# Fewer unread products in the opening, an earlier exp table, and batch 2 loaded through the software queue

## The chip, the cores and the metric

The kernel runs on one core of one Trainium2 chip. The metric is the time of one execution on the device in microseconds (us); before the change it was 310.43 us, the median of 8 runs (309.83 to 311.7).

The core has a matrix engine (TensorE, PE in the profile), VectorE (DVE), ScalarE (ACT), GpSimd (POOL) and SyncE (SP). Each works through its own list of instructions in order and waits for the others by semaphores. Sixteen DMA engines move data; GpSimd issues transfers into a software queue, which can also change float32 to bfloat16 on the way, and SyncE into a hardware queue, which can also transpose.

## The reference

Two stages follow each other. The first is attention over q, k and v of shape 8 x 8 x 576 x 64 (batches, heads, tokens, head size), in float32. For heads 0 to 3 a token sees itself and the 31 before it; for heads 4 to 7 it sees itself and every earlier token at a distance that 32 divides:

```python
mask_local = (rel >= 0) & (rel < stride)
mask_strided = (rel >= 0) & (pos[None, :] % stride == pos[:, None] % stride)
scores = np.where(masks[None, :, :, :], scale * q @ k^T, -1e9)
attn = softmax(scores);  x = (attn @ v) as 4608 tokens x 512
```

The second is a two-layer network over the 4608 tokens: `h = x @ w_in` (512 to 2048), Mish (`h * tanh(log1p(exp(h)))`), and `g @ w_out` (2048 to 512).

## The kernel before

**Blocks.** The tokens pass through the network in nine blocks of 512, t = 0 to 8. For each block `mlp1` makes the hidden layer in 8 groups of two 128-wide columns, 8 matmuls each (L557), and ScalarE applies Mish to each group (L563). `mlp2` makes the output (L580) in 16 pieces of 4 matmuls. Between the pieces of `mlp2` of block t stand the steps of the attention of batch t+1, written out by hand in `attn_steps` as a list `at`: the steps of `at[i]` follow piece i. So the order on TensorE is the order of the calls; there is no scheduler.

**Attention of a batch.** The strided heads ("s") are cut into 8 groups of 72 tokens, the local heads ("l") into 6 windows of 96 tokens. `qk` makes scores in a pair of PSUM banks (`acc`, three pairs in all) and ScalarE takes their exp (L339), which needs the exp table: ScalarE holds one table at a time, and Exp and Mish lie in different ones. `mask` multiplies by the mask on VectorE (L347). `pv` and `pv2` multiply by v, whose 65th column is ones, so that the sum of the weights comes along; VectorE divides by it (L374, L375; in `pv2` L388, L389). `xt` transposes the result on TensorE and copies it into `xT`, the input of `mlp1`. Batches 0 and 1 also have their q and k transposed on TensorE (`t_step`, `t_step_loc0`), with a copy out of PSUM behind each; the transposes share two small PSUM buffers (`tile_t`) with `pv`. From batch 2 on, q and k are transposed by DMAs of SyncE (`str_by_dma`, `loc_by_dma`).

**The opening.** Batch 0's attention runs before any block. TensorE has little to do there, and between its steps stand calls of `fill` (L526): products of a zeroed tile `kTs[1]` that nobody reads, 512 columns each. There are seven calls with 9, 4, 2, 2, 4, 2 and 2 products. The first waits for the memset of `kTs[1]` (L629).

**Loads.** GpSimd issues the loads of batches 0 and 1, of all weights, and of the strided q and k of every batch, in the order of the calls. A transfer that it issues waits for the eighth transfer before it. In the program of before, batch 2's local q and k and its v come by SyncE in float32 (`load_qk_loc`, `load_v`), and GpSimd casts them (`cast_qk_loc`, `cast_v`). A small transfer `gate` (L718), which reads a piece of `w_out`, stands ahead of them in SyncE's queue and so holds them back until that piece of `w_out` has landed. Behind them in the same queue stand the six transposing transfers of batch 2 (called in `at[9]` of block 0), and behind these the output of block 0 and the loads of batch 3. The function `next_loads`, called in `at[2]` of block 0, holds GpSimd's part: a copy of rows of v of batch 1 (windows overlap by 32 rows), the casts of batch 2 and the loads of batch 3's strided q and k.

**Block 0.** Its pieces run with `fc_major`, so that the four 128-token tiles of the output are all open at once and hold two PSUM pairs. The scores of batch 1 have only the third pair: the next part of the scores can start when exp has read the last.

Of the kernel before, what the change touches and what calls it, by code (L numbers as in the profile page):

```python
# [11 lines left out]
BF16 = mybir.dt.bfloat16  # L12
AF = mybir.ActivationFunctionType
# [4 lines left out]
WQ = 96  # L18
CL, PL = 6, 96
SU = 80  # L20
CS, PN = 8, 72
# [19 lines left out]
def kernel(ctx, tc, q, k, v, moe_w_in, moe_w_out, out):  # L41
    nc = tc.nc
    B, H, S, D = q.shape
# [9 lines left out]
    const = ctx.enter_context(tc.tile_pool(name="const", bufs=1))  # L53
    w_in = const.tile([128, 4, DF], BF16, name="w_in")
    w_out = const.tile([128, 16, DM], BF16, name="w_out")
# [11 lines left out]
    ql = [const.tile([128, CL, 4, D], BF16, name=f"ql{i}") for i in range(2)]  # L67
    kl = [const.tile([128, CL, 4, D], BF16, name=f"kl{i}") for i in range(2)]
    qs = [const.tile([128, 4, CS * D], BF16, name=f"qs{i}") for i in range(2)]
    ks = [const.tile([128, 4, CS * D], BF16, name=f"ks{i}") for i in range(2)]  # L70
    vl = [const.tile([128, NW, 4, D + 1], BF16, name=f"vl{i}") for i in range(2)]
# [4 lines left out]
    kTs = [const.tile([128, 16 * SU + 48], BF16, name=f"kTs{i}") for i in range(2)]  # L76
    P_s = [const.tile([PN, 2, n * PN + 56], BF16, name=f"Ps{i}") for i, n in enumerate((7, 7, 4))]
    P_l = [const.tile([128, 2, n * WQ + 32], BF16, name=f"Pl{i}") for i, n in enumerate((5, 5, 2))]
    gate = const.tile([1, 256], BF16, name="gate")
    x_l = const.tile([128, NW, 256], BF16, name="x_l")  # L80
    x_s = const.tile([128, CS, 256], BF16, name="x_s")
    xs_t = const.tile([128, CS, 2, 96], BF16, name="xs_t")
# [12 lines left out]
    def tile_t(name):  # L95
        return ps_t.tile([128, 512], F32, tag="pt", name=name)
# [18 lines left out]
    def load_qk_loc(b):  # L115
        for dst, src in ((kl32, k), (ql32, q)):
            nc.sync.dma_start(
                dst[0:PL].rearrange("p h i d -> p (h i) d"),
                src[b, 0:4].rearrange("h (i p) d -> p (h i) d", p=PL),
            )  # L120
# [6 lines left out]
    vsd = [vsd[:, 2048 * i:2048 * i + 2048] for i in range(2)]  # L127

    def load_v_str01(b):
        dst = vsd[b].rearrange("p (h x) -> p h x", h=4)  # L130
        if b == 0:
            load_str01(dst, v, b)
        else:
            nc.gpsimd.dma_start(dst, v[b, 4:8].rearrange("h (p j) d -> p h (j d)", j=CS))

    def load_v_loc01(b, w0, w1):
        for w in range(w0, w1):
            nc.gpsimd.dma_start(
                vl[b][32:128, w, :, 0:D], v[b, 0:4, WQ * w:WQ * w + WQ].rearrange("h p d -> p h d")
            )  # L140

    def rows_v_loc01(b, w0, w1, eng):
        w0 = max(w0, 1)
        cast(eng, vl[b][0:32, w0:w1, :, 0:D], vl[b][96:128, w0 - 1:w1 - 1, :, 0:D])

    def copy_v_str01(b, eng, j0, j1):
        cast(
            eng, vs[b][0:PN, :, j0:j1, 0:D],
            vsd[b].rearrange("p (h j d) -> p h j d", h=4, j=CS)[:, :, j0:j1, :],
        )  # L150

    def load_v_str(b):
# [9 lines left out]
    def load_v(b):  # L162
        load_v_str(b)
        load_v_loc(b)
# [13 lines left out]
    def cast(eng, out_, in_):  # L178
        if eng is nc.scalar:
            nc.scalar.copy(out_, in_)  # L180
        else:
            eng.tensor_copy(out_, in_)  # L182

    def cast_qk_loc(b, e_k, e_q):
        for e, dst, src in ((e_k, kl, kl32), (e_q, ql, ql32)):
            to = by_tile(dst[b % 2])
            for hp in range(2):
                cast(
                    e, to[:, hp].rearrange("p i e d -> p e i d"), src[0:PL, 2 * hp:2 * hp + 2]
                )  # L190

    def by_tile(x):

        return x[0:PL].rearrange("p j h d -> p (j h d)").rearrange(
            "p (t i e d) -> p t i e d", t=2, i=NW, e=2
        )
# [16 lines left out]
    def cast_v(b, e_s, e_l):  # L213
        cast(e_s, vs[b % 2][0:PN, :, :, 0:D], vs32[0:PN])
        cast_v_loc(b, e_l)
# [33 lines left out]
    def t_step_loc0(src, dst, hp, eng):  # L249

        tr = tile_t("tr")[:].bitcast(BF16)
        for j in range(CL):
            for e in range(2):
                nc.tensor.transpose(  # L254
                    tr[64 * e:64 * e + 64, PL * j:PL * j + PL], src[0:PL, 2 * hp + e, j, :],
                    ident[0:PL, 0:PL],
                )
        cast(
            eng, dst.rearrange("c (p j) -> c p j", j=CL),
            tr[:, 0:S].rearrange("c (j p) -> c p j", j=CL),  # L260
        )
# [5 lines left out]
    def t_steps1():  # L267
        r = [lambda w=w, hp=hp: t_step(1, w, hp) for hp in range(2) for w in ("k", "q")]
        kq = [
            (x[:].rearrange("p h (j d) -> p h j d", d=D), d)  # L270
            for x, d in ((rows(kl[1]), kTl[:, :, 32:32 + S]), (rows(ql[1]), qTl[:]))
        ]
        return r + [
            lambda x=x, d=d, hp=hp: t_step_loc0(x, d[:, hp, :], hp, nc.vector)
            for hp in range(2) for x, d in kq
        ]


# [247 lines left out]
    def fill(t, n):  # L526

        for _ in range(n):
            nc.tensor.matmul(  # L529
                t[:, 0:512], lhsT=kTs[1][:, 512:640], rhs=kTs[1][:, 0:512], start=True, stop=True  # L530
            )

    def fill_acc(i, n):
        fill(acc(i, "fill")[:, 0, :], n)
# [82 lines left out]
    with tc.manual_schedule():  # L617
# [8 lines left out]
        load_v_str01(0)  # L626
        load_qk_loc01(0, kl0, ql0)
        kl0, ql0 = [x.rearrange("p h (j d) -> p h j d", d=D) for x in (kl0, ql0)]
        Dv.memset(kTs[1][:], 0.0)  # L629
        Dv.memset(vl[0][:, :, :, D:D + 1], 1.0)  # L630
        Dv.memset(vl[0][0:32, 0], 0.0)
        load_v_loc01(0, 0, 3)
# [20 lines left out]
                )  # L653

        a = Attn(0)
        fill_acc(2, 9)
        for hp in range(2):
            t_step(0, "k", hp, Sc if hp else Dv)
        a.bias("s", 0, 0)
# [1 line left out]
        for hp in range(2):  # L661
            t_step(0, "q", hp, Sc if hp else Dv)
        a.bias("s", 1, 1)
        fill_acc(2, 2)
        a.bias("s", 2, 2)
        for i in range(3):
            a.qk([("s", i)], i)
# [5 lines left out]
        t_step_loc0(kl0, kTl[:, 1, 32:32 + S], 1, Sc)  # L673
        a.pv2("s", 2, 1)
        a.pv2("s", 4, 2)
        fill_acc(0, 4)
        t_step_loc0(ql0, qTl[:, 0, :], 0, Sc)
        t_step_loc0(ql0, qTl[:, 1, :], 1, Sc)
        a.pv2("s", 6, 0)
        a.bias("l", 0, 1)  # L680
        fill(tile_t("fill"), 2)
        a.bias("l", 1, 2)
        a.qk([("l", 0)], 1)
        a.qk([("l", 1)], 2)
# [6 lines left out]
        load_v_str01(1)  # L691
        load_qk_loc01(1, rows(kl[1]), rows(ql[1]))
        load_w_out(1, 3)
        for h in range(4):
            nc.gpsimd.dma_start(
                vl[1][32:128, :, h, 0:D], v[1, h].rearrange("(w p) d -> p w d", p=WQ)
            )
        load_w_out(3, 4)
        a.bias("l", 2, 0)
        a.qk([("l", 2)], 0)  # L700
        a.xt("s", 0, Dv)
        a.xt("s", 1, Dv)
        Sc.preload_act_table(AF.Mish)
        fill(tile_t("fill"), 2)
        a.pv2("l", 0, 1)
        a.pv2("l", 2, 0)
        a.pv2("l", 4, 1)
# [5 lines left out]
        a.xt("l", 1)  # L713
        Dv.memset(vl32[0:32], 0.0)
        for x in (ks, qs):
            Po.memset(x[0][64:SU], 0.0)
        load_qk_str(2)
        nc.sync.dma_start(gate[:], w_out[0:1, 11, 0:256])  # L718
        load_qk_loc(2)

        def next_loads():
            rows_v_loc01(1, 0, 6, Po)
            load_v(2)
            cast_qk_loc(2, Po, Po)
            load_qk_str(3)
            cast_v(2, Po, Po)

        for t in range(NBLK):
            x, y, z = accs
            if t > 0:  # L730
                gT, g1 = mlp1(t, accs)
            ts, at, a1 = [], [], []
            if t == 0:
                ts, at = t_steps1(), attn_steps(1, y, y)
                at[2] += [lambda: copy_v_str01(1, nc.vector, 0, CS), next_loads] + ts[4:6]
                at[3] += ts[6:8]
                at[9] += [lambda: str_by_dma(2), lambda: loc_by_dma(2)]
                out_accs, accs = (z, x), (y, z, x)
            else:
                if t <= 2:  # L740
                    at = attn_steps(t + 1, x, y, z if t == 2 else None)
                elif t + 1 < B:
                    a1 = str_steps(t + 1)
                    at = loc_steps(t + 1, x, y)
                if t == 1:
                    at[9].append(lambda: str_by_dma(3))
                if t == 2:
                    Dv.memset(x_s[64:96], 0.0)
                if t + 2 < B:
                    at[9].append(lambda: loc_by_dma(t + 2))  # L750
                if 1 < t < B - 3:
                    at[9].append(lambda: str_by_dma(t + 3))
                out_accs, accs = (z, y), (z, x, y)
            for i, g in enumerate(g1):
                g()
                if i < len(a1):
                    for s in a1[i]:
                        s()
                if t == 0:
                    for n in {6: (0, 1), 7: (2, 3)}.get(i, ()):  # L760
                        ts[n]()
            if t > 0 and t + 2 < B:
                cast_qk_loc(t + 2, Po, Po)
                if 1 < t < B - 3:
                    load_qk_str(t + 3)
                if t < 3:
                    cast_v(t + 2, Po, Po)
                else:
                    at[5].append(lambda: cast_v(t + 2, Po, Po))
            if t == 1:  # L770
                load_qk_str(4)
            if t == NBLK - 1:
                mlp2_last(t, gT, (z, y, x))
                break
            for i, g in enumerate(mlp2(t, gT, out_accs, fc_major=(t == 0))):
                g()
                if i < len(at):
                    for s in at[i]:
                        s()
            if t + 3 < B:  # L780
                load_qk_loc(t + 3)
                if t == 1:
                    str_by_dma(4)
                load_v(t + 3)
# [30 lines left out]
```

## Time and profile before

| | |
|---|---|
| median of 8 runs | 310.43 us |
| the profiled execution | 309.83 us |
| its span, first to last instruction | 308.10 us |
| TensorE busy in the span | 297.2 us (96%) |
| ScalarE, VectorE, GpSimd busy | 181.0, 155.5, 101.8 us |
| first product of `mlp1` that runs on without a wait | 23.78 us |
| `mlp2` of block 0 with attention of batch 1 | 36.9 to 59.99 us |
| `mlp2` of block 1 with attention of batch 2 | 73.81 to 92.47 us |
| transposing transfers of batch 2, first to last issue | 55.33 to 72.17 us |

Times in the profile are microseconds from the first instruction, unless ns is written. A line of the timeline gives the start, the length, the engine, the line of the kernel, the operation, what it writes and reads, its shape and how often it follows itself; in brackets stands how long the engine had been idle before it, and what ended the idle time. PEld is TensorE's weight load. SPq and the DMA lines of POOL are issues of transfers, whose data lands later. Matmuls are pipelined and their ends are modelled, so a matmul's line looks longer than the time by which it moves the next.

### The profile page before, as it was taken

Reading aid. Unit: us, or ns where it says so; the run is one execution under the profiler, and the core shown is the slowest. Engines: PE = TensorE matmul, PEld = TensorE weight load, DVE = VectorE, ACT = ScalarE, POOL = GpSimd, SP = SyncE. Lnnn points to the kernel's source line nnn. Section 1 sums busy time; section 2 is a strip of 40 time slices with the busy share of each in tenths; the row PEclk is TensorE's granted clock in tenths of the full one; section 3 lists DMA queues with packets and bytes.
Section 4 is the critical chain, followed back from the end, with each engine's and each line's share of the span. In section 5 each row is a group of like instructions: output and inputs, shape, how many; then the busy total and the mean of one; then the engine's idle time right before and its main releaser. Section 6 shows DMA issues by size and latency. Waiting matters only on the chain.

```text
span 308.1 us, 5881 instructions
## 1 busy us (share of the span) xinstructions
PE 297.2 (96%) x2437; PEld 154.7 (50%) x2437; DVE 155.5 (50%) x375; ACT 181.0 (59%) x193; POOL 101.8 (33%) x116
## 2 busy tenths in 40 slices
PE   6989979999999999999999999999999999999995
PEld 2544545544554455444579654445444544444444
DVE  3670257400870066578787978797879850000000
ACT  5555533667537664768766876687668746216501
POOL 8782551660236024502790297028600000000000
PEclk9999999999999999999999999999999999999999
DMA  7999999998999999999979996898420120011011
GB/s 115 175 185 201 204 169 174 183 147 210 186 192 147 206 155 208 187 197 193 168 160 168 194 177 149 146 190 148 126 89 0 41 98 0 2 68 68 0 70 68
DMA packets 97346, 42.84 MB, mean 139 GB/s; under 512 B 79400, under 2 KB 91112, under 8 KB 97320
## 3 DMA queue, kind: packets, MB, share of 16 engines
q1 hardware_dynamic: 78856, 30.94, 55.8%
q0 software_dynamic: 18176, 11.28, 27.7%
q8 instruction: 19, 0.31, 0.5%
q10 hardware_dynamic: 288, 0.25, 0.3%
q14 instruction: 7, 0.06, 0.1%
HBM read 36.82 MB, written 9.44 MB: 150 GB/s over the span
## 4 chain that ended last, share of the span: by engine, by line
PE 90%; DVE 4%; DMA 2%; ACT 1%; issue 1%; POOL 1%; ACTq 0%; POOLq 0%
PE psh L557 40%; PE pso L580 34%; PE po L363 5%; PE pso L607 5%; PE ps L325 3%; DMA qs<-in_q_dram 2%; DVE x_l L375 1%; DVE x_s L375 1%; PE fill L529 1%; PE trx L402 1%; ACT Ps L339 1%; PE ps L298 1%; PE tr L238 1%; PE tr L254 1%; DVE rden L374 1%
## 5 line engine op out<-in xcount | busy, mean ns | idle before, releaser
L557 PE MATMUL psh<-xT,w_in 128*128 128x512 bf16 (+1 forms) x640 | 130.6, 358 | 1.0 <-ACT xT L180 0.7
L580 PE MATMUL pso<-w_out,gT 128*128 128x512 bf16 x512 | 121.7, 379 | 0.0
L563 ACT ACTIVATE gT<-psh 128x1024 bf16<-128x1024 f32 x72 | 72.4, 1023 | 47.3 <-PE psh L557 47.3
L557 PEld LDWEIGHTS <-w_in 128*128 128x128 bf16 x640 | 60.1, 98 | 56.5 <-issue 1.4
L580 PEld LDWEIGHTS <-gT 128*128 128x128 bf16 x512 | 45.4, 97 | 46.0
L182 POOL CAST kl<-kl 96x768 bf16<-96x768 f32 x12 | 9.9, 846 | 76.8 <-DMA kl<-in_k_dram 60.9
L437 DVE STREAM_TRANSPOSE xs_t<-x_s 32x512 bf16<-32x512 bf16 x48 | 33.7, 702 | 0.9
L587 ACT COPY osb<-pso 128x1024 f32<-128x1024 f32 x16 | 17.6, 1100 | 24.6 <-PE pso L580 14.0
L374 DVE RECIPROCAL rden<-po 72x4 f32<-72x4 f32 (+1 forms) x98 | 17.3, 176 | 26.2 <-PE po L363 26.0
L347 DVE TENSOR_TENSOR Ps<-Ps,consts_sb 72x864 bf16<-72x864 bf16 (+3 forms) x12 | 7.0, 583 | 41.7 <-ACT Ps L339 41.7
L428 DVE STREAM_TRANSPOSE xT<-x_l 32x384 bf16<-32x384 bf16 x48 | 27.3, 569 | 0.7
L182 DVE COPY osb<-pso 128x512 f32<-128x512 f32 (+1 forms) x2 | 1.1, 558 | 51.3 <-PE pso L607 51.3
L339 ACT ACTIVATE Ps<-ps 72x864 bf16<-72x864 f32 (+3 forms) x21 | 17.4, 860 | 13.3 <-PE ps L325 13.3
L375 DVE TENSOR_TENSOR x_s<-po,rden 72x256 bf16<-72x256 f32 x56 | 23.5, 420 | 1.9
L444 ACT COPY xT<-xs_t 128x576 bf16<-128x576 bf16 x8 | 21.4, 2941 | 0.0
L363 PEld LDWEIGHTS <-Ps 72*128 72x128 bf16 x256 | 14.9, 97 | 11.6 <-DVE Ps L347 0.8
L182 POOL CAST vl<-vl 128x768 bf16<-128x768 f32 (+2 forms) x24 | 18.5, 771 | 4.9 <-DMA vl<-in_v_dram 3.8
L339 ACT ACTIVATE Pl<-ps 128x960 bf16<-128x960 f32 (+1 forms) x20 | 17.1, 875 | 3.8 <-PE ps L325 3.8
L375 DVE TENSOR_TENSOR x_l<-po,rden 96x256 bf16<-96x256 f32 x42 | 17.6, 420 | 1.4
L180 ACT COPY xT<-trx 128x576 bf16<-128x576 bf16 x14 | 8.8, 639 | 15.4 <-PE trx L412 11.2
L363 PE MATMUL po<-vs,Ps 72*128 72x65 bf16 x256 | 17.4, 194 | 0.1
L182 POOL CAST ql<-ql 96x768 bf16<-96x768 f32 x12 | 10.3, 882 | 14.2 <-DMA ql<-in_q_dram 14.2
(86 smaller groups left out, 233.8 us busy)
## 6 DMA issues: line engine op xcount, KB each, us to landing
out_dram<-osb SPq DMA_DIRECT2D x16, 512.0 KB, 4.6
kl<-in_k_dram SPq DMA_DIRECT2D x6, 576.0 KB
ql<-in_q_dram SPq DMA_DIRECT2D x6, 576.0 KB, 11.6
vs<-in_v_dram SPq DMA_DIRECT2D x6, 576.0 KB
vl<-in_v_dram SPq DMA_DIRECT2D x6, 576.0 KB, 10.0
w_out<-in_moe_w_out_dram POOLq DMA_DIRECT2D x4, 512.0 KB, 15.2
ks<-in_k_dram POOLq DMA_DIRECT2D x7, 288.0 KB, 7.3
qs<-in_q_dram POOLq DMA_DIRECT2D x7, 288.0 KB, 8.4
```

Source lines behind the costliest of these rows:

```text
L182: eng.tensor_copy(out_, in_)
L339: nc.scalar.activation(pt[0:n, :, 0:nw], t[0:n, :, o0:o0 + nw], AF.Exp, scale=scale)
L363: nc.tensor.matmul(po[:, h, :], lhsT=pt[0:n, c0:c0 + 128], rhs=rhs, start=True, stop=True,)
L374: nc.vector.reciprocal(rden[0:m, :], po[0:m, :, D])
L375: nc.vector.tensor_tensor(out=dst.rearrange("p (h d) -> p h d", h=4), in0=po[0:m, :, 0:D], in1=rden[0:m, :].unsqueeze(2).to_broadcast([m, ...
L428: nc.vector.transpose(dst[32 * q:32 * q + 32, :, :, m:m + 32], src[m:m + 32, :, :, q, :])
L437: nc.vector.transpose(xs_t[32 * q:32 * q + 32, :, :, m:m + 32], src[m:m + 32, :, :, q, :])
L444: nc.scalar.copy(xT[:, 2 + c, t0:t0 + S].rearrange("p (n j) -> p j n", j=CS), xs_t[:, :, c, 0:PN])
L557: nc.tensor.matmul(ps[:, u, o:o + n], lhsT=w_in[:, cc, fc * 128:(fc + 1) * 128], rhs=xT[:, cc, a:a + n], start=(cc == 2 and o == 0), stop= ...
L563: nc.scalar.activation(gT[:, 2 * g:2 * g + 2, :], ps[:], AF.Mish)
L580: nc.tensor.matmul(p[:, ot % 2, :], lhsT=gT[:, fc, 128 * ot:128 * ot + 128], rhs=w_out[:, fc, :], start=(fc == 0), stop=(fc == 15),)
L587: nc.scalar.copy(osb[:], p[:])
```

## The change

It has three parts. In the opening, the memset of `kTs[1]` is cut in two, of which the first covers what `fill` reads; the numbers of unread products become 11, 4, 1, 2 and 1, and two calls go; the second copy of `xt("s", ...)` of batch 0 moves from VectorE to ScalarE. In block 0 the exp table is loaded behind piece 0 of `mlp2`, the copy of v and `next_loads` move from `at[2]` to `at[1]`, ahead of the mask, and the copies of the local q transposes of batch 1 move from VectorE to ScalarE. Batch 2's local q and k and its v are loaded by GpSimd's queue as bfloat16: the loads of q and k are one transfer for each head, and those of v are the functions of batch 1, which now take any batch. The gate, the float32 loads of batch 2 and its casts go; what stays on GpSimd is a copy of v's strided rows and the row copy. The memsets of the padding rows of `ks[0]` and `qs[0]` move from GpSimd to VectorE.

```diff
-    gate = const.tile([1, 256], BF16, name="gate")
...
+    def load_v_loc_h(b):
+        for h in range(4):
+            nc.gpsimd.dma_start(
+                vl[b % 2][32:128, :, h, 0:D], v[b, h].rearrange("(w p) d -> p w d", p=WQ)
+            )
...
-            lambda x=x, d=d, hp=hp: t_step_loc0(x, d[:, hp, :], hp, nc.vector)
-            for hp in range(2) for x, d in kq
+            lambda x=x, d=d, hp=hp, e=e: t_step_loc0(x, d[:, hp, :], hp, e)
+            for hp in range(2) for (x, d), e in zip(kq, (nc.vector, nc.scalar))
...
-        Dv.memset(kTs[1][:], 0.0)
+        Dv.memset(kTs[1][:, 0:640], 0.0)
+        Dv.memset(kTs[1][:, 640:], 0.0)
...
-        fill_acc(2, 9)
+        fill_acc(2, 11)
...
-        fill_acc(2, 2)
+        fill_acc(2, 1)
...
-        fill_acc(0, 4)
+        fill_acc(0, 1)
...
         a.bias("l", 0, 1)
-        fill(tile_t("fill"), 2)
         a.bias("l", 1, 2)
...
-        for h in range(4):
-            nc.gpsimd.dma_start(
-                vl[1][32:128, :, h, 0:D], v[1, h].rearrange("(w p) d -> p w d", p=WQ)
-            )
+        load_v_loc_h(1)
...
-        a.xt("s", 1, Dv)
+        a.xt("s", 1)
         Sc.preload_act_table(AF.Mish)
-        fill(tile_t("fill"), 2)
...
-            Po.memset(x[0][64:SU], 0.0)
+            Dv.memset(x[0][64:SU], 0.0)
         load_qk_str(2)
-        nc.sync.dma_start(gate[:], w_out[0:1, 11, 0:256])
-        load_qk_loc(2)
+        rows_v_loc01(1, 0, 6, Po)
+        for dst, src in ((kl, k), (ql, q)):
+            to = by_tile(dst[0])
+            for h in range(4):
+                nc.gpsimd.dma_start(
+                    to[:, h // 2, :, h % 2, :], src[2, h].rearrange("(i p) d -> p i d", p=PL)
+                )
+        load_v_str01(2)
+        load_v_loc_h(2)

         def next_loads():
-            rows_v_loc01(1, 0, 6, Po)
-            load_v(2)
-            cast_qk_loc(2, Po, Po)
             load_qk_str(3)
-            cast_v(2, Po, Po)
+            copy_v_str01(2, Po, 0, CS)
+            rows_v_loc01(2, 0, 6, Po)
...
-                at[2] += [lambda: copy_v_str01(1, nc.vector, 0, CS), next_loads] + ts[4:6]
+                at[0] += [lambda: Sc.preload_act_table(AF.Exp)]
+                at[1] += [lambda: copy_v_str01(1, nc.vector, 0, CS), next_loads]
+                at[2] += ts[4:6]
```

More of the change, by code (lines that the diff above doesn't have):

```diff
@@ L129, in load_v_str01 @@
     def load_v_str01(b):
-        dst = vsd[b].rearrange("p (h x) -> p h x", h=4)
+        dst = vsd[b % 2].rearrange("p (h x) -> p h x", h=4)
         if b == 0:
@@ L140, in load_v_loc01 @@
             )
+    def load_v_loc_h(b):
[3 more added lines that the diff above has]
+            )
     def rows_v_loc01(b, w0, w1, eng):
-        w0 = max(w0, 1)
-        cast(eng, vl[b][0:32, w0:w1, :, 0:D], vl[b][96:128, w0 - 1:w1 - 1, :, 0:D])
+        w0, x = max(w0, 1), vl[b % 2]
+        cast(eng, x[0:32, w0:w1, :, 0:D], x[96:128, w0 - 1:w1 - 1, :, 0:D])
     def copy_v_str01(b, eng, j0, j1):
         cast(
-            eng, vs[b][0:PN, :, j0:j1, 0:D],
-            vsd[b].rearrange("p (h j d) -> p h j d", h=4, j=CS)[:, :, j0:j1, :],
+            eng, vs[b % 2][0:PN, :, j0:j1, 0:D],
+            vsd[b % 2].rearrange("p (h j d) -> p h j d", h=4, j=CS)[:, :, j0:j1, :],
         )
```

## The prediction

> **What bounds the kernel now.** I read the page's busy shares first, then a table of busy time by stage, then the list of waits of TensorE alone, then the timeline where that table shows TensorE idle. The busy share names the engine:
>
> ```profile
> PE 297.2 (96%) x2437; PEld 154.7 (50%) x2437; DVE 155.5 (50%) x375; ACT 181.0 (59%) x193; POOL 101.8 (33%) x116
> ```
>
> TensorE fills 96% of the span, and all matmuls of the nine token blocks stay as they are. So a gain has to come from the 4% in which TensorE stands still, or from TensorE work without a reader. In the table of stages (columns: stretch; then busy of PE, PEld, DVE, ACT, POOL; granted clock; DMA) the stretches to look at are these:
>
> ```profile
> 10.00:20.00 10.00, 8.91 (x186) 5.74 (x184) 6.57 (x15) 7.22 (x10) 8.55 (x13) 1.00 1.48 172
> 20.00:23.80 3.80, 2.69 (x29) 1.64 (x30) 3.26 (x6) 1.46 (x3) 1.77 (x3) 1.00 1.24 207
> ...
> 37.00:60.00 23.00, 20.99 (x256) 11.81 (x253) 14.90 (x41) 10.10 (x13) 10.77 (x11) 1.00 1.42 179
> 60.00:73.80 13.80, 13.80 (x65) 6.27 (x64) 0.00 (x0) 9.24 (x9) 6.33 (x7) 1.00 1.03 151
> ```
>
> From 60 us on a stage is full (13.80 of 13.80). Before 24 us, and from 37 to 60 us, it is not; and part of what counts as busy before 24 us is the fill, which nobody reads. The timeline (start, length, engine, operation, idle before and its releaser) of the opening:
>
> ```profile
> 13.05 1.03 PE L529 MATMUL fill<-kTs 128*128 128x512 bf16 x4
> ...
> 15.31 0.59 PE L529 MATMUL fill<-kTs 128*128 128x512 bf16 x2
> ...
> 17.70 1.42 DVE L182 COPY xT<-trx 128x576 bf16<-128x576 bf16 x2 [1.65 <-PE trx L412]
> 18.51 0.59 PE L529 MATMUL fill<-kTs 128*128 128x512 bf16 x2 [0.59 <-DVE xT L182]
> ...
> 20.38 0.43 PE L363 MATMUL po<-vl,Pl 128*128 128x65 bf16 x8 [0.76 <-DVE x_l L389]
> ```
>
> Here a fill stands in TensorE's order ahead of work that could run: the last pair waits until VectorE has emptied a transpose buffer (18.44), and the local attention products behind it start only at 18.94. Then the first block's second projection:
>
> ```profile
> 36.59 1.02 ACT L563 ACTIVATE gT<-psh 128x1024 bf16<-128x1024 f32 x1 [1.23 <-PE psh L557]
> 39.19 1.28 ACT L339 ACT_TABLE_LOAD   x1 [1.58 <-PE ps L325]
> 40.49 0.89 ACT L339 ACTIVATE Ps<-ps 72x864 bf16<-72x864 f32 x1
> 41.42 0.37 PE L325 MATMUL ps<-qTs,kTs 64*128 64x72 bf16 x12 [1.35 <-ACT Ps L339]
> 42.53 0.75 DVE L182 COPY kTl<-tr 128x576 bf16<-128x576 bf16 x1
> 43.20 0.74 DVE L182 COPY qTl<-tr 128x576 bf16<-128x576 bf16 x1
> ```
>
> ScalarE is free from 37.61, but loads the exp table only when the scores are there (39.19). TensorE's next scores need the same PSUM pair, so TensorE stands 1.35 us.
>
> **The opening, part by part.** The first fill group grows from 9 to 11, and the memset it waits for is halved. Memsets of 664 and 64 words took 612 and 112 ns, 0.83 ns a word, so 320 words take about 325 ns: the fill starts at 0.95+0.33+0.06 = 1.34 instead of 1.62. Nine fills took 1.62 to 5.28, less the last's tail: loads 0.427 us apart. Eleven at that pace end at 1.34+11x0.427 = 6.03; the first keys release TensorE at 6.06. Cost 0.0, at most 0.1. The 4 and the 2 fills that stay are hidden by the query transfer and the first exp.
>
> Fill 2 to 1 before the third bias: the bias pair shares the fill's PSUM pair and started at 9.82, when the second fill had drained. One fill less is 0.22; the last query copy (to 9.64) does not bind. First exp: 10.56 to 10.34, and the chain behind moves 0.22.
>
> Fill 4 to 1 at 13.05: the local query transposes (14.01) then wait for their buffer, which VectorE's copy of the keys frees (12.81+0.74 = 13.55, less 0.22 = 13.33). They start near 13.38, 0.63 earlier. The fill pair at 15.31 goes: the bias behind it needs VectorE's read of a product (14.53+0.69 = 15.22, less 0.22 = 15.00), so it starts about 15.05 instead of 15.74, 0.69 earlier; the query copies, also 0.63 earlier, end at 15.05. The three local exps then run 15.98 to 18.19 (16.67 and 2.21 long before).
>
> The fill pair at 18.51 goes, and the second xT copy moves from VectorE to ScalarE. The first pair of products runs as soon as exp and transposes are done (17.1). VectorE has one copy (17.0 to 17.7) ahead of its division instead of two, and divides until 17.72+0.20+0.04+0.69 = 18.65. The second pair needs the third exp (18.19). The third pair needs the first division: 18.7 instead of 20.38. On ScalarE the moved copy runs 18.19 to 18.83 (0.64, its row elsewhere), then the Mish table to 20.11, before the next xT copy (about 20.5). From the third pair on the order of TensorE is the old one, with the same links (VectorE 0.88 per product, one transpose, one ScalarE copy): MLP1's free run starts at about 22.15 instead of 23.78. **Opening: -1.6.**
>
> Does the input keep up? Each transfer that GpSimd issues waits for the eighth before it, so its waits date the landings: w_in chunks by 21.4, 23.9, 26.7, batch 1's keys 29.2 and queries 31.5, first w_out chunk 33.3. Needed after the shift: about 23.9, 27.3, 30.8, 32.5, 32.7 and 35.3. All hold, the tightest by about 1 us.
>
> [...] In the row, the first nine fills stand 427 ns apart, the four at 6.94 217 ns ((1.03-0.38)/3): TensorE begins at half pace. [...] By the row, TensorE stayed fast from 17.2 to 20.65, with 1.3 us of matmuls that aren't transposes in 3.4 us. After the change the thinnest such stretch, 16.35 to 19.75, holds about 1.5 (products 0.97, projection 0.6). I take the row: it stays fast, cost 0. [...]
>
> **The first block's second projection.** The exp table is put behind the last Mish: 37.61 to 38.89, before the scores end at 39.1. Exp starts at 39.19 instead of 40.49: -1.3. The copy of vs (0.69) runs before exp instead of after the mask, its data since 35.3 there. The two qTl copies go to ScalarE (0.64 each), which is idle from 42.78 to 46.51 in the old trace. On old times less 1.3: VectorE copies kTl at 40.7 to 41.45, so the first product no longer waits for it (41.97, was 43.33); the next transposes start behind it at 42.3 (were 44.00), the last at 43.0, after VectorE's division (were 44.54). The projection's next piece starts 1.56 earlier. The rest is in old order: **-1.55**.
>
> **Batch 2.** Off SP: the gate and four loads. Off GpSimd: two memsets (1.80 each; VectorE does them at half the words in its idle after 23.6), four casts of k, q, and five of v. On GpSimd now: 13 transfers (8 of k and q per head, 1 vs, 4 vl), all issued behind the row copy of vl, which waits for batch 1's values. That copy ended at 48.4. At 0.72 an issue the last of q is issued at 54.2, vs at 54.9, vl at 57.8, batch 3's keys and queries behind. Bytes read and rows moved are the same, and they share the engines with SP's six transposes, which now start when keys and queries of batch 2 are in (about 49 to 51, was 55.3). With the landings of the old per-head vl row (13.2) the last q is there at 67.4 and the last transpose (1.22 to issue, 2.6 to land) at 71 to 72; the first local scores of batch 2 would be due at 79.11-3.15 = 76.0, the strided ones at 72.3 (issue of theirs: 8.27+4.33 from 51, so 64 and 5.9 to land, 70). vs lands by 54.9+15.4 = 70.3 and needs one GpSimd copy (cast 1.89): 72.2, due at 77.76-3.15 = 74.6. All with landings from the most crowded time; with shorter ones the margin is 5 to 10 us. So cost 0; the cover is this margin of 2 us in the pessimistic reading.
>
> [...] One GpSimd issue of queries took 1.19 instead of 0.72 (at 41.67), beside VectorE's copy of vs. [...] By the row the price is 0.47, once; were all 13 hit, +6.1 on GpSimd, and vs would be ready at 76 to 78, up to 3.5 us late. The vs copy has moved away from the issues, and VectorE's other work there reads PSUM or takes 0.4 to 0.6, so I take 0.
>
> **Sum.** -1.6-1.55 = -3.15. The profiled execution took 309.83 (span 308.10 and 1.73 around it): it becomes 306.7, span 304.95. The median shown is 310.43, 0.6 above the profiled one; I predict the median: 310.43-3.15 = 307.3. About 0.3% (0.9 us) is what a measurement of this kernel can tell from no change.
>
> **Rivals.** [...] (b) The opening is hidden: the input, not the order, sets MLP1's start or a chunk of w_out comes late; then 1 us is given back at 42 (the queries' issue that waits for w_out's second chunk was done at 42.86; the chunk is due at 44.92+0.07-3.15 = 41.85): 308.3. For: the DMA engines are 90% busy to 64 us. (c) Slower: batch 2's vs comes late. Place: the first product of batch 2, due 74.6. Each us that its copy ends later costs one; from 77.8 on the gain is gone, from 78.7 the kernel is slower by more than 0.3%: ended at 80, it gives 312.7. For: 13 small-row transfers behind each other, mixed with transposes. Against: the same rows passed through full engines before and were in by 63.86 (the cast of vl). (d) The change does half of what it says in the second projection: VectorE, not the exp, sets the transposes' order, only 0.8 of the 1.55: 308.0.
>
> **Numbers.** Forecast 0.62, (d) 0.10, (b) 0.09, (a) 0.10, (c) 0.05, and 0.04 for no change by a mix. Range: below, 4.2 saved if also the waits at 52 to 54 us shrink: 306.2; above, (a) with 0.1 more: 309.0. Of (a), 0.06 is faster, 0.03 the same and 0.01 slower, as its cost goes from 1.7 to 3.4. So faster 0.62+0.10+0.09+0.06 = 0.87, same 0.03+0.04 = 0.07, slower 0.05+0.01 = 0.06.
>
> **What the new profile would show.** The fill starting near 1.34; the free run of MLP1 at about 22.2; no wait of TensorE's scores for exp in the second projection, table load right after the last Mish at about 36; the end of that stage at about 56.8 instead of 59.99; no wait of TensorE in the next block; from there the old lengths. Wrong it would be by fills or projections 427 ns apart after 17 us, by a wait of TensorE for kTl, qTl or vs near 70 to 78, or by a stage after 60 us that is longer than before.

## The result and the profile after

The changed kernel takes 306.94 us, the median of 11 runs, against 310.83 us for the kernel before it on the same chip (32 runs): a ratio of 0.9871, with a 95% interval of 0.9845 to 0.9897. The forecast was 307.3 us. The profiled execution took 306.98 us, with a span of 305.2. (One run of 311.58, in which TensorE's mean granted clock was 0.994, is not in the ratio.)

The page's busy shares: TensorE is busy for 297.2 us as before, with six matmuls fewer, and its busy time is now 97% of the span. So the 2.9 us that the span lost are idle time of TensorE (10.9 us before, 8.0 now).

```profile
PE 297.2 (97%) x2431; PEld 154.7 (51%) x2431; DVE 156.0 (51%) x375; ACT 182.7 (60%) x196; POOL 101.5 (33%) x120
```

The table of stages of the changed kernel (columns as in the prediction). The first stretch ends 2.66 us earlier than that of 37 to 60 us before, and starts 2.60 earlier, still in MLP1:

```profile
34.40:57.34 22.94, 21.97 (x272) 12.48 (x271) 14.26 (x39) 11.67 (x15) 12.95 (x18) 1.00 1.57 163
57.34:71.14 13.80, 13.80 (x65) 6.27 (x64) 0.00 (x0) 9.25 (x9) 4.72 (x5) 1.00 1.85 132
```

TensorE stood still for 0.97 us in the 22.94 us of the first row; the row of before had 2.01 in 23.00. From 57.34 us, which was 59.99, it is full as it was.

The timeline of the opening after the change:

```profile
12.93 0.38 PE L534 MATMUL fill<-kTs 128*128 128x512 bf16 x1
...
17.11 0.76 DVE L187 COPY xT<-trx 128x576 bf16<-128x576 bf16 x1 [1.18 <-PE trx L417]
17.17 0.43 PE L368 MATMUL po<-vl,Pl 128*128 128x65 bf16 x8
18.16 0.66 ACT L185 COPY xT<-trx 128x576 bf16<-128x576 bf16 x1
18.34 0.85 PE L368 MATMUL po<-vl,Pl 128*128 128x65 bf16 x16 [0.74 <-ACT Pl L344]
...
22.16 4.04 PE L562 MATMUL psh<-xT,w_in 128*128 128x512 bf16 x18 [0.73 <-ACT xT L185]
```

One unread product stands where four stood, and those at 15.31 and 18.51 are gone. The local products run at 17.17 and 18.34 and are not released by VectorE's copies any more. MLP1 runs on from 22.16 us (23.78 before).

The timeline of block 0's second projection after the change:

```profile
34.96 1.02 ACT L568 ACTIVATE gT<-psh 128x1024 bf16<-128x1024 f32 x1 [1.23 <-PE psh L562]
36.01 1.28 ACT L741 ACT_TABLE_LOAD   x1
37.59 0.89 ACT L344 ACTIVATE Ps<-ps 72x864 bf16<-72x864 f32 x1 [0.30 <-PE ps L330]
38.52 0.37 PE L330 MATMUL ps<-qTs,kTs 64*128 64x72 bf16 x12
...
42.07 1.02 PE L585 MATMUL pso<-w_out,gT 128*128 128x512 bf16 x4 [0.28 <-DMA w_out<-in_moe_w_out_dram]
...
48.07 1.25 POOL L187 COPY vl<-vl 32x1280 bf16<-32x1280 bf16 x1 [4.71 <-DMA vl<-in_v_dram]
48.68 1.15 DVE L352 TENSOR_TENSOR Pl<-Pl,consts_sb 128x960 bf16<-128x960 bf16 x1
50.98 0.30 PE L368 MATMUL po<-vl,Pl 128*128 128x65 bf16 x4 [0.24 <-DVE x_l L380]
```

The table is loaded straight behind the last Mish, and TensorE's scores at 38.52 no longer stand 1.35 us for exp. Two things are new and cost time: the projection at 42.07 waits 0.28 us for the second chunk of `w_out`, and the mask at 48.68 takes 1.15 us (0.64 before), beside GpSimd's row copy. Together the stage, counted from MLP1's free run, has become 36.21 - 35.18 = 1.03 us shorter (59.99 - 23.78 before, 57.34 - 22.16 now), not 1.55.

So 1.62 + 1.03 = 2.65 us are won by 57.34 us, and the span is 308.1 - 305.2 = 2.9 us shorter. What is won at the start is still there at the end. That this needs the third part of the change was the surprise of the experiments.

### The profile page after: what moved, and what is told of

The parts are those of the page before. It is cut to its first block, busy times and chain, and to the rows that moved or that the text cites. A ratio compares the mean times of both kernels' runs of the same rounds, so it can differ in the third digit from the quotient of the medians.

```text
span 305.2 us, 5875 instructions
## 1 busy us (share of the span) xinstructions
PE 297.2 (97%) x2431; PEld 154.7 (51%) x2431; DVE 156.0 (51%) x375; ACT 182.7 (60%) x196; POOL 101.5 (33%) x120
## 4 chain that ended last, share of the span: by engine, by line
PE 81%; DMA 11%; DVE 3%; POOL 2%; issue 1%; ACT 0%; POOLq 0%
PE psh L562 36%; PE pso L585 33%; DMA w_out<-in_moe_w_out_dram 6%; PE pso L612 5%; PE po L368 4%; DMA w_in<-in_moe_w_in_dram 3%; PE ps L330 3%; DMA lq<-in_q_dram 2%; DVE x_l L380 1%; DVE x_s L380 1%; DVE Pl L352 1%; PE trx L407 1%; DVE rden L379 1%; POOL w_in L172 0%; POOL ks L110 0%
## 5 line engine op out<-in xcount | busy, mean ns | idle before, releaser
L187 POOL CAST kl<-kl 96x768 bf16<-96x768 f32 x10 | 8.4, 862 | 63.7 <-DMA kl<-in_k_dram 55.1
L185 ACT COPY xT<-trx 128x576 bf16<-128x576 bf16 x15 | 9.5, 640 | 14.0 <-PE trx L417 11.4
L187 POOL CAST vl<-vl 128x768 bf16<-128x768 f32 (+2 forms) x20 | 15.4, 772 | 4.1 <-DMA vl<-in_v_dram 3.2
L352 POOL TENSOR_TENSOR Ps<-Ps,consts_sb 72x1008 bf16<-72x1008 bf16 (+1 forms) x9 | 14.5, 1647 | 1.1 <-ACT Ps L344 1.0
## 6 DMA issues: line engine op xcount, KB each, us to landing
ks<-in_k_dram POOLq DMA_DIRECT2D x7, 288.0 KB, 10.9
```

The lines of the kernel that those rows point to most:

```text
L352: meng.tensor_tensor(out=pm, in0=pm, in1=mk[0:n, :].unsqueeze(1).unsqueeze(1).to_broadcast([n, 2, nu, w]), op=ALU.mult,)
```

## The experiments

All ratios are to the kernel before, run on the same chip at the same time. Spans, starts and waits are those of one profiled execution of each kernel. It is not always at the kernel's median: with the opening alone it is 2.0 us faster, with the first eleven and four unread products 1.2 us slower. So an account in spans explains profiles, and the medians only as far as they agree with it.

### One part at a time

First the opening alone: the kernel before, with the memset cut in two, the new numbers of unread products and the second copy of `xt` on ScalarE.

> The kernel before with the opening's edits alone (memset in two, 11/4/1/2/1 unread products, second xT copy on ScalarE). Theory (each part gives its own): MLP1 runs on without a wait from about 22.2 us instead of 23.78, and 1.6 us less in all, ratio 0.995. Rival (the input sets the pace behind it, so that the opening's gain is given back in the first block): the start is at 22.2 too, but the end of the first block's second projection is moved by less than 1.2 us and the time by under 0.8 us.

Measured: ratio 0.9985 (0.9957 to 1.0013), which is not told apart from no change; 0.995 was expected. The span is 307.2. MLP1 starts to run on at 22.07 us and the gain is 1.66 us still at 90.81, the start of block 2's MLP1. In block 4's MLP1, which also holds the strided attention of batch 5, it is 0.89 (a point at 166.23 before stands at 165.34). The timeline shows where the rest went: the first of these products waits for GpSimd's cast of `vs`:

```profile
156.13 1.89 POOL L182 CAST vs<-vs 72x2048 bf16<-72x2048 f32 x1
...
158.07 0.28 PE L363 MATMUL po<-vs,Ps 72*128 72x65 bf16 x4 [0.60 <-POOL vs L182]
```

Then block 0 alone: the early exp table, the copy of `vs` ahead of the mask and the `qTl` copies on ScalarE.

> The kernel before with the first block's edits alone (exp table behind the last Mish, copy of v ahead of the mask, local q copies on ScalarE). Theory as predicted: the second projection of block 0 ends 1.55 us earlier, ratio 0.995. Rival (as the profile of the full change suggests, something else takes the place of the wait): 1.0 us or less, and a new wait of TensorE or a stretched VectorE operation in this stage names it.

Measured: ratio 0.9965 (0.9943 to 0.9987), span 307.1. Block 0 ends 1.49 us earlier and block 1 1.48; in block 3's MLP1 only 0.93 is left, and the span is 1.0 us shorter. Here the loss is in the second projection of block 2, by the timeline:

```profile
112.10 2.26 POOL L182 CAST kl<-kl 96x768 bf16<-96x768 f32 x2 [12.62 <-DMA kl<-in_k_dram]
112.39 1.02 DVE L347 TENSOR_TENSOR Ps<-Ps,consts_sb 72x576 bf16<-72x576 bf16 x1
...
115.56 0.29 PE L363 MATMUL po<-vl,Pl 128*128 128x65 bf16 x4 [0.38 <-DVE rden L374]
```

GpSimd's pair of casts (1.59 us otherwise) and VectorE's mask (0.45 otherwise) begin within 0.3 us of each other, both take longer, and VectorE is late for TensorE.

Then the third part alone, batch 2's loads through the software queue.

> The kernel before with batch 2's loads through GpSimd's queue alone, with the old opening and the old first block. Theory: no change, 0.0 within 0.3 us, since all of batch 2 is in time either way. Rival one (the new loads delay the first block: a late piece of w_out, or GpSimd's row copy beside VectorE's mask): slower by 0.3 to 0.8 us. Rival two (they help later stages): faster by 0.3 us, all of it after 60 us.

Measured: ratio 0.9988 (0.9965 to 1.0012), span 308.0; the starts of MLP1 in blocks 1 and 2 and the point in block 4 lie within 0.13 us of before. Alone this part is worth nothing that can be measured.

Last the first two parts together, without the third.

> The full change without batch 2's part: opening and first block alone. Theory: 3.0 us less than before, the same as the full change. Rival one (batch 2's new loads cost 0.3 to 0.8): 3.3 to 3.7 us less. Rival two (the shift of 3 us needs the earlier loads of batch 2): a wait of TensorE for kTs, kTl or vs of batch 2 between 70 and 80 us, and only 2 us less or fewer.

Measured: ratio 0.9930 (0.9904 to 0.9956), span 306.2. Up to block 1's MLP1 this is the prediction to the hundredth: MLP1 from 22.20, block 0 ended at 56.84, 3.15 us earlier; the block's own gain is 1.57. At the point in block 4's MLP1 (164.37) 1.86 are left: about the 2 us of the second rival, but lost in block 4 and not at a wait between 70 and 80 us. The ratio's interval lies above that of the full change (0.9845 to 0.9897): the part that gives nothing alone gives 0.993 - 0.9871 = 0.6%, 1.8 us, on top of the others. Between the two spans it is 1.0 us, with 0.54 us lost in block 0 of the full change's profiled execution that the other did not lose (see the section on the mask).

### The cause: GpSimd's cast in block 3

The timelines around block 3's second projection for three kernels. First before: the issue of the load of batch 5's keys on SP (its queue), GpSimd's chain, and TensorE's first product, in block 4's MLP1, with the `vs` that GpSimd has cast.

```profile
136.19 0.47 SPq L117 DMA_DIRECT2D kl<-in_k_dram  x1
...
147.93 1.88 POOL L182 CAST ql<-ql 96x768 bf16<-96x768 f32 x2 [2.93 <-DMA ql<-in_q_dram]
...
151.26 4.85 POOL L347 TENSOR_TENSOR Ps<-Ps,consts_sb 72x1008 bf16<-72x1008 bf16 x3
156.05 1.89 POOL L182 CAST vs<-vs 72x2048 bf16<-72x2048 f32 x1
...
158.96 0.28 PE L363 MATMUL po<-vs,Ps 72*128 72x65 bf16 x4
```

The same with the first two parts of the change:

```profile
135.77 0.48 SPq L117 DMA_DIRECT2D kl<-in_k_dram  x1
...
150.37 4.85 POOL L347 TENSOR_TENSOR Ps<-Ps,consts_sb 72x1008 bf16<-72x1008 bf16 x3
155.16 1.89 POOL L182 CAST vs<-vs 72x2048 bf16<-72x2048 f32 x1
...
157.10 0.28 PE L363 MATMUL po<-vs,Ps 72*128 72x65 bf16 x4 [1.11 <-POOL vs L182]
```

And with the full change:

```profile
133.35 1.28 SPq L116 DMA_DIRECT2D kl<-in_k_dram  x1
...
148.62 4.85 POOL L352 TENSOR_TENSOR Ps<-Ps,consts_sb 72x1008 bf16<-72x1008 bf16 x3
153.41 1.89 POOL L187 CAST vs<-vs 72x2048 bf16<-72x2048 f32 x1
...
156.30 0.28 PE L368 MATMUL po<-vs,Ps 72*128 72x65 bf16 x4
```

Before, the cast of `vs` ended at 156.05 + 1.89 = 157.94 and was needed at 158.96: 1.0 us of slack, in a chain that runs from the landing of the queries (by SP's queue) over two casts, two issues and three masks. With the first two parts TensorE comes 3 us sooner, but SP issues the keys only 0.4 us sooner and the cast ends 0.9 us sooner; the slack is used up and 1.1 us are waited. With the third part SP is rid of batch 2's loads and the gate: its load of batch 3's keys is issued at 67.71 us (74.58 before), that of batch 5's still 2.8 us sooner, and the cast ends 2.6 us sooner, in step with TensorE. The slack is 1.0 us again.

What the third part does by itself stands in the profile of the kernel that has it alone:

```profile
132.84 0.47 SPq L116 DMA_DIRECT2D kl<-in_k_dram  x1
...
153.94 1.88 POOL L187 CAST vs<-vs 72x2048 bf16<-72x2048 f32 x1
...
159.08 0.29 PE L368 MATMUL po<-vs,Ps 72*128 72x65 bf16 x4
```

There TensorE comes as late as before, and the cast ends at 155.82: the slack is 3.3 us instead of 1.0. So the part shortens no wait of TensorE when it is alone, and makes room for what the other two win.

If this is the cause, the wait must go when the cast of `vs` is put ahead of the three masks, with nothing else changed. This was done from block 3 on, for the kernel with the first two parts and for the full change:

```diff
-                    at[5].append(lambda: cast_v(t + 2, Po, Po))
+                    at[5].insert(2, lambda: cast(Po, vs[t % 2][0:PN, :, :, 0:D], vs32[0:PN]))
+                    at[5].append(lambda: cast_v_loc(t + 2, Po))
```

> Opening and first block alone, and from block 3 on GpSimd casts vs before its three masks instead of behind them. Theory (without batch 2's new loads the shift ends at block 4, where the first product waits 1.11 us for that cast at the end of GpSimd's list): the wait is gone, the first product is near 156 us, and the time falls by about 1.1 us, to 0.990 of before. Rival (the loss is some effect of the DMA engines on all later blocks): the wait moves elsewhere and the time stays at 0.993.

Measured: ratio 0.9892 (0.9856 to 0.9929), span 304.9. The timeline of this kernel:

```profile
150.64 1.89 POOL L182 CAST vs<-vs 72x2048 bf16<-72x2048 f32 x1
152.58 4.83 POOL L347 TENSOR_TENSOR Ps<-Ps,consts_sb 72x1008 bf16<-72x1008 bf16 x3
...
155.83 0.29 PE L363 MATMUL po<-vs,Ps 72*128 72x65 bf16 x4
```

The wait is gone, the point in block 4's MLP1 comes at 163.10 instead of 164.37, and the span is 1.3 us shorter. At 140.55 us, in block 3's second projection, TensorE begins the same products in both profiles, so the 1.27 us arise behind it, where the wait of 1.11 was. The intervals of the two ratios overlap; what shows the cause is the pair of profiles.

> The full change with vs cast before the masks. Theory: there the cast ends 1.0 us ahead of its product, so no change against the full change (0.987 of before, within 0.002). Rival (the cast binds in many executions of the full change too): faster by 0.5 us or more, and less spread.

Measured: ratio 0.9872 (0.9842 to 0.9902), span 304.6; the same as the full change within its interval. Where the slack is there already, no gain of the order is seen.

### Which edit of the opening counts

The full change with the old numbers of unread products, 9, 4, 2, 2, 4, 2 and 2; the moved copy and the cut memset stay.

> The full change with the old counts of unread products (9, 4, 2, 2, 4, 2, 2); the moved copy, the halved memset and the rest stay. Theory: 1.2 to 1.5 us of the opening's 1.6 are the fills', so MLP1 runs on from about 23.4 instead of 22.2 us and the time is 0.991 of before. Rival (the copy moved to ScalarE gives most of it): start below 22.7.

Measured: ratio 0.9947 (0.9922 to 0.9973), MLP1 from 23.77 us: all of the opening's 1.6 us go (1.2 to 1.5 were expected). Now the other way round, the new numbers with only the second `xt` copy back on VectorE:

```diff
-        a.xt("s", 1)
+        a.xt("s", 1, Dv)
```

> The changed kernel with the second copy of batch 0's strided result back on VectorE; the fills stay as changed. Theory of the prediction: behind two copies of 0.74 VectorE's first local division ends 0.74 later, so the third pair of products and with it MLP1's free run start 0.6 to 0.75 later, at 22.8 to 22.9, and the time is 0.7 above the changed kernel, ratio 0.989. Rival: the division isn't what MLP1 waits for, because the third exp (ends 18.3) and the table load set the rest of the opening; then 22.16 stays and the ratio is 0.987.

Measured: MLP1 from 22.60 us, 0.44 later than with the full change, where 0.6 to 0.75 was expected; span 305.1, ratio 0.9917 (0.9889 to 0.9945; three of its six runs had a granted clock of 0.993 to 0.994, of which more at the end). VectorE's two copies hold its first division back from 17.79 to 18.23. But this profile reached the first copy 0.22 us sooner than the full change's (16.89 and 17.11). Counted from there, MLP1 runs on after 5.71 us; in the full change, and in five more kernels with the copy on ScalarE, it is 5.05. So the copy's share is 0.66, as the prediction had it, and it has it only once the unread products are gone.

### How little work keeps TensorE's clock

The prediction took it that TensorE stays fast without most of the unread products. To test what carries that, only the first eleven were kept.

> The full change with the first 11 unread products only; the later four calls (4, 1, 2, 1) are left out. Theory (TensorE stays at full pace by its own work): the start of MLP1's run at 22.0 to 22.2 us, projections 216 ns apart from there, same time as the full change within 0.3 us. Rival (the remaining ones keep the clock up): a stretch of matmuls 427 ns apart between 10 and 26 us, and 1 us or more lost.

Measured: ratio 0.9922 (0.9896 to 0.9948), mean granted clock 0.982 in the profiled execution, MLP1 from 24.26 us, 2.1 later than with the full change, and later than the 23.78 of the kernel before. My theory, that TensorE's own work keeps it fast, fell: by half microseconds the granted clock is 0.50 from about 9.2 to 19.4 us. Ahead of the fall, from 5.8 to 9.2 us, TensorE was busy for 2.35 us, more than half of it with transposes (two groups of 0.68), and stood still for 1.06 at most at a time. Which of these brought the fall is not shown. Next the first two calls, 11 and 4:

```diff
-        fill_acc(2, 1)
...
-        fill(tile_t("fill"), 2)
...
-        fill_acc(0, 1)
```

> The changed kernel with only its first two calls of fill, 11 and 4 products; the 1, 2 and 1 behind them go. Theory: what keeps TensorE at full pace is the four products near 8 us, in the wait for the query transfer; the later three calls stand among other matmuls and aren't needed. Then the products of MLP1 that run without a wait start at 22.0 to 22.2, as in the changed kernel (22.16), the bias pair of 128x480 stays at 0.57, and the time is that of the changed kernel, ratio to before 0.987. Rival: the later calls are needed as well; then some matmuls between 10 and 19 us stand at half pace, MLP1 runs from 23 to 24.3, and the ratio is 0.990 to 0.993.

Measured: ratio 0.9926 (0.9897 to 0.9955), MLP1 from 24.81 us, later than the rival's 23 to 24.3, but by the half pace that it named. The table by stretches of 2 us of this kernel (the third figure from the right is the granted clock):

```profile
10.00:12.00 2.00, 0.60 (x19) 0.34 (x11) 1.15 (x3) 2.00 (x3) 0.89 (x2) 1.00 1.44 171
12.00:14.00 2.00, 1.60 (x34) 1.48 (x35) 0.97 (x2) 0.47 (x2) 0.67 (x1) 0.58 1.78 178
14.00:16.00 2.00, 2.00 (x43) 1.79 (x41) 1.69 (x4) 1.02 (x3) 1.81 (x3) 0.50 1.18 94
16.00:18.00 2.00, 2.00 (x16) 0.72 (x15) 0.89 (x2) 0.41 (x1) 2.00 (x4) 0.50 1.29 159
```

And of the full change, with one unread product at 9.26, two at 10.66 and one at 12.93:

```profile
10.00:12.00 2.00, 1.88 (x55) 1.25 (x56) 0.92 (x3) 1.56 (x3) 1.28 (x3) 1.00 1.54 187
12.00:14.00 2.00, 1.83 (x63) 1.56 (x55) 1.93 (x5) 1.20 (x4) 1.12 (x2) 1.00 1.78 177
```

The two rows from 14 to 18 us look like a well used TensorE, 2.00 of 2.00; but at a granted clock of 0.50 the same work takes longer: 24 transposes take 1.17 us at 14.50 (0.70 at 13.48 in the full change). The fall comes after a stretch, 9.43 to 12.40, with 32 scores, eight products and otherwise nothing. The missing products are not all of it: in this profile the local keys landed late, TensorE waited 1.15 us for them and began their transposes at 12.40 (11.73 in the full change). So some 0.7 us of the 2.65 by which MLP1 is late can be the landing's, and whether the clock would have fallen here without it is not shown; one of the seven runs kept 1.0. The kernel with eleven alone has no such wait, and all twelve of its runs had a lower clock.

### The table and the copies in block 0

The full change without the early table load:

```diff
-                at[0] += [lambda: Sc.preload_act_table(AF.Exp)]
```

> The changed kernel without the early load of the exp table; the copy of batch 1's v ahead of the mask and the copies of qTl on ScalarE stay. Theory of the prediction: the table load moves back in front of the first exp of block 0, which starts 1.3 later, and all but 0.25 of the block's gain is lost: the block ends at 58.4 to 58.8 instead of 57.3, the time is 1.0 to 1.3 above the changed kernel, ratio 0.991. Rival: the moved copies carry a good part of the gain by themselves, since VectorE, not exp, released the transposes: the block ends at 57.6 to 58.0 and the ratio is 0.988 to 0.989.

Measured: ratio 0.9928 (0.9901 to 0.9955). The timeline of this kernel has the old wait back:

```profile
37.25 1.28 ACT L344 ACT_TABLE_LOAD   x1 [1.58 <-PE ps L330]
38.54 0.89 ACT L344 ACTIVATE Ps<-ps 72x864 bf16<-72x864 f32 x1
...
39.48 0.37 PE L330 MATMUL ps<-qTs,kTs 64*128 64x72 bf16 x12 [1.35 <-ACT Ps L344]
```

From MLP1's free run to the end of the stage it takes 57.76 - 21.84 = 35.92 us, against 36.21 before and 34.64 with all of the block's edits (the kernel without the third part; the full change with the cast ahead of the masks has the same). So the table is worth 1.28 us, the length of its load in the first line, and the moved copies 0.29. The working of the prediction had 1.3 and 0.25.

### The mask beside GpSimd's copy

In the full change's profile the mask took 1.15 us beside the row copy. The row copy of batch 1 in five pieces:

```diff
-        rows_v_loc01(1, 0, 6, Po)
+        for w in range(1, 6):
+            rows_v_loc01(1, w, w + 1, Po)
```

> The changed kernel with GpSimd's copy of rows of batch 1's v in five copies of a fifth of the size, one for each window. [...]

Measured: ratio 0.9898 (0.987 to 0.9927), where 0.986 was expected; it is not told apart from the full change. In the profiled execution batch 1's values landed 1.8 us sooner, so the pieces had nearly ended when the 128x960 mask began, and it took 0.65. So the run does not test whether short copies spare that mask. A smaller one did run beside the pieces; this kernel's timeline:

```profile
46.30 2.09 POOL L187 COPY vl<-vl 32x256 bf16<-32x256 bf16 x5 [5.46 <-DMA vl<-in_v_dram]
46.38 0.35 DVE L352 TENSOR_TENSOR Pl<-Pl,consts_sb 128x384 bf16<-128x384 bf16 x1
```

It has its usual length, but here VectorE was first: its mask before this one had begun at 46.02. The five pieces took 2.09 us, the undivided copy of the full change 1.25; whether a mask that begins beside short copies keeps its usual length is not shown. Beside an undivided copy that began first, in the kernel with the first two parts, a mask of usually 0.45 us takes 1.21:

```profile
45.63 1.25 POOL L182 COPY vl<-vl 32x1280 bf16<-32x1280 bf16 x1 [3.60 <-DMA vl<-in_v_dram]
45.98 1.21 DVE L347 TENSOR_TENSOR Ps<-Ps,consts_sb 72x576 bf16<-72x576 bf16 x1
```

The copy ends at 46.88 and the mask at 47.19, 0.31 later. In four more kernels the same two meet, with 0.31, 0.32, 0.32 and 0.32 (old numbers of unread products, eleven and four, only eleven, block 0 alone). The 128x960 mask of the full change ends 0.51 behind its copy. Each is the mask's usual length less 0.13 or 0.14, though the two ran beside each other for 0.64 to 1.13 us. So the mask ends as if all but about 0.14 us of its work stood behind the copy, an estimate from these lengths; what holds it up is not shown. What it costs depends on the moment at which batch 1's values land: in the kernel with the first two parts the longer mask (1.21 us) cost TensorE nothing (the stage took the same 34.64 us as with the divided copy). In the profiled execution of the full change TensorE fell behind that kernel by 0.35 us at the second chunk of `w_out` and by 0.19 more behind the mask. The full change with the cast ahead of the masks is the same program up to block 3; in its profile neither happened, and the stage took 34.64. So the 0.54 belongs to the landings of one execution.

## Why the prediction was right, and where it was not

**Opening, -1.6.** Measured -1.62, with MLP1 at 22.16 for the predicted 22.15, and the fill at 1.26 for 1.34. The links held within about 0.1 us as they were followed: the products, then the moved copy for its share. The 0.1 is at the eleven products: in this execution TensorE came to full pace only behind the key transposes (1.14 us at 5.95; 0.68 before), and the query transposes began at 8.38 instead of 8.28.

**The clock, cost 0.** The result held: from 7.3 us TensorE is at full pace (the four unread products there take 1.03 us, as before), and the granted clock is 1.00. (The clock's column reads 1.00 ahead of that too, where the unread products stand 427 ns apart; so the start is read from the pace.) The reason given did not hold. The prediction looked for the thinnest stretch at 16.35 to 19.75 and called the kept fills "hidden". Hidden they are, but they carry the clock: without the kept products behind the first eleven the granted clock is 0.50 from about 9.2 to 19.4 us, and with only four of them from about 12.3 to 19.15; the working never weighed what stands ahead of these falls. The cost of 1.7 to 3.4 us that the numbers and the top of the range put on (a), a fall of TensorE's clock, is shown by no run; what the runs show is MLP1 2.1 us later with the first eleven alone (24.26 for 22.16) and 2.65 later with eleven and four. How much work is enough is not shown: with the first eleven alone the clock fell though from 5.8 us on TensorE had not stood still for longer than 1.06 us.

**Second projection of block 0, -1.55.** -1.57 in the kernel with the first two parts and -1.03 in the profiled execution of the full change. The 0.54 between them is 0.35 for the second chunk of `w_out`, the wait that rival (b) placed at 42 us with a price of 1, and 0.19 behind the longer mask (1.15 us for 0.64); other executions of the same stage lost neither. What GpSimd and VectorE cost each other was weighed in the prediction for GpSimd's issues only (1.19 us instead of 0.72, once), and taken as 0; it came at another instruction, a mask of VectorE beside GpSimd's row copy (1.15 us). Rival (d) falls: VectorE's order gives what was worked out.

**Batch 2, cost 0, and "from there the old lengths".** This is the step that failed. Its margin was sound: the `vs` copy ended at 65.46 and was due at 75.11, a margin of 9.6 us (the pessimistic reading had 2), so rival (c) falls. But the sum carried 3.15 us from 60 us to the end over a stage with a slack of 1.0 us, at GpSimd's cast of `vs` in block 3, which the profile of before showed and the working did not look at. By the prediction's own steps the first two parts alone would give all of the 3.15; they give 1.9 in the span. The part costed at 0 is what keeps the rest. The total is right by luck here: this part moved SP's and GpSimd's chain by about as much as the others moved TensorE, which the prediction had not seen.

**The sum.** -3.15 was predicted; 2.9 was measured in the span, 3.9 between the medians. The 1.0 between these two is in no link of the prediction: the profiled execution of the full change is at its own median (306.98 and 306.94), that of before is 1.0 below its median of 32 runs, and what makes those runs slower than the profiled one is not shown. As a ratio the forecast, 307.3 to 310.43, is 0.9899, just above the measured interval.

## What to carry to other kernels

A gain at the start reaches the end only if every engine's chain moves with it: ahead of the sum, go through the later stages and look for the smallest distance between the end of what another engine or queue supplies and the instruction that needs it, and compare it with the gain. An edit that gives nothing alone can be what lets another's gain through, so test it by leaving it out as well as by itself. Before work without a reader is cut, look at what it does besides filling time: here the eight that were kept behind the first eleven are worth 2.1 us by the clock.

## What the hardware showed unexpectedly

The mean granted clocks of the runs with only eleven unread products lie in three groups, at 0.994, 0.988 to 0.989 and 0.982 to 0.983, in spans of 305.5 to 308.7 us. If the clock was 0.50 for a part of the span and 1.00 for the rest, that is half pace for about 3.7, 6.7 to 7.4 and 10.4 to 11.0 us, an estimate from the clocks and spans. In stretches of half a microsecond the profile with eleven and four shows 12.3 to 19.15 us, 6.8, and that with eleven alone 9.2 to 19.4, 10.2. What sets these lengths is not shown. Executions of one kernel differ: with eleven and four products, one of seven kept 1.0 and took 306.38 us, one had 0.994 and 307.62, and the five at 0.987 to 0.989 took 308.37 to 309.71. The kernel with the `xt` copy back on VectorE was at 1.0 in three runs of six and at 0.993 to 0.994 in the others, 306.9 to 307.84 against 308.47 to 309.37 us. The changed kernel was at 0.998 to 1.0 in eleven of twelve runs. Over all runs whose clock is on record, the kernels with the new numbers of unread products had 0.992 to 0.995 in 8 of 71, and those with the old ones in 4 of 111: more often with the new numbers, but that difference was not tested. In which stretch the clock of the unprofiled runs fell, and what decides it, was not measured.

What stays open: the kernel before, and those with the divided row copy and without the early table load, ran 1.0, 1.5 and 0.9 us slower in the median than in their profiled executions, the latter two at a full clock in every run, and no profile shows where.
